# A planned one-core kernel: clearing, identity copy and running products moved in the opening, features due one step earlier, six float32 steps instead of eight

## The chip, the cores and the metric

The kernel runs on one core of one Trainium2 chip. The core has five engines with a program each: TensorE (PE in the profile), VectorE (DVE), ScalarE (ACT), GpSimd (POOL) and SyncE (SP), which here only issues transfers. The metric is the time of one execution on the device, in microseconds. Before the change the median of 3 runs is 601.78 us (600.33 to 602.82).

## The reference

Three layers follow each other. The first is a linear attention over 4 sequences of 768 tokens with 8 heads: in chunks, the decay between two tokens is the exponential of a difference of running sums of log a, and a state of 16 by 32 per head is carried from chunk to chunk. The other two are layers of 3072 tokens with 256 inputs, 2048 inner features and 256 outputs, one with softplus and one with a piecewise square.

```python
log_a = np.log(np.clip(a, 1e-06, 1.0))
cum = np.cumsum(la, axis=-1)
L = np.exp(cum[:, :, :, None] - cum[:, :, None, :])       # causal part only
y_intra = np.einsum('bhij,bhjd->bhid', CB * L, xc)
y_inter = np.einsum('bhin,bhnd->bhid', Cc, state) * decay_to_i[:, :, :, None]
state = decay_full[:, :, None, None] * state + np.sum(Bx, axis=2)
...
g = np.maximum(h, 0.0) + np.log1p(np.exp(-np.abs(h)))     # first layer, h = x @ w_in
g = np.where(pos, h, np.where(neg, 0.0, (h + beta) ** 2 / (4.0 * beta)))   # second
return (g @ w_out).astype(np.float32)
```

All inputs are float32 and the weights are given as 64-bit words, so that the kernel itself rebuilds float32 weights from two 32-bit halves.

## The kernel before

**Tiling.** The kernel takes its own chunks of 128 tokens: 6 chunks of 4 sequences, so 24 units, u = 4 c + b. A unit of chunk 0 makes its decays from the running sums (spread on TensorE, an exponential on ScalarE, L759). A unit of a later chunk loads rows of a and takes running products of them with one long scan on VectorE (`decay`, L757). `weigh` (L802) multiplies the scores by the decays, `out` (L826 to L838) makes outputs and state on TensorE, `evac` (L851) copies the output as high half xh on ScalarE, and `ready` (L860) subtracts it to give the low half xl on VectorE. A unit's xh and xl are its features.

**The layers as steps.** A step is an `up` (12 products of 256 columns, L893 to L895: xh by wih, xh by wil, xl by wih), an activation (`g`, L917), and a `down` into an accumulator. In chunks 0 and 1 a step takes 256 tokens (two units) and 256 of the 2048 inner features; later 512 tokens and 128 features. A `down` is either whole (L946: the float32 activation by the float32 weight, 4 products, which the trace shows as 8) or split: `g_hi` copies the high half (L500 on ScalarE or L502 on VectorE), `g_lo` subtracts (L932, on VectorE or GpSimd), and 12 products follow (L958). `whole(s)` says which: steps 0 to 7 before the change.

**The weights.** A piece of the first layer is loaded into one of 4 buffers st (two pieces go through the space of later features, raw), and rebuilt by w0 (L562 or L566), w1 (L574, ScalarE), w2 (L586), w3 (L598), a copy of the high half (L500 or L502) and `split_w` (L608) for the low half. wih, wil, woh and wol are the halves of the in and out weights. The names carry buffer numbers in the instruction lists: wih_75 to wih_82 are the eight pieces of w_in, woh_91 to woh_98 those of w_out.

**What sets the order.** Nothing is scheduled at run time. `program()` lists jobs with an engine, a cost, what they need, and the buffers they take and give back. `Jobs.order` walks through them: among the jobs that could start first on an engine it takes the one due earliest. A due time runs back from what follows; the job ("ready", u) has its own, `when(first step of its tokens - LEAD)`. Each engine then runs its list in that order, waiting in place. Short matmuls on an idle tile (L1034) are put in where the planner sees TensorE waiting in the opening; they write the bank of the job behind them.

**The opening (L987 to L1026, and the jobs of `a`).** GpSimd makes an identity (eye3), its seven copies (L1023), and the 0/1 patterns for the spread (L1018, L1022). `clip_a`, `log`, `sums` and `terms` (L640 to L657) make the running sums of chunk 0. `clip` (L687) writes the clipped a with zeros in its first column, `store` puts it in DRAM for the rows of the later chunks, and `runs` (L704, L707) takes running products of all of a, which `store_runs` and the loads `dec` bring to where `cd` (L777) and the state update need them, from chunk 1 on.

Of the kernel before, what the change touches and what calls it, by code (L numbers as in the profile page):

```python
# [14 lines left out]
NB, H, S, D, N = 4, 8, 768, 32, 16  # L15
Q = 128
# [6 lines left out]
PE, ACT, DVE, POOL, SP = "PE", "ACT", "DVE", "POOL", "SP"  # L23
# [167 lines left out]
def program():  # L191

    jobs = Jobs()
    add = jobs.add
# [29 lines left out]
    add("clip_load", SP, 400, due=-1e5, takes=["t"], size=98e3)  # L224
    add("clip", DVE, 350, needs=["clip_load", "sums"])
    add("store", SP, 800, needs=["clip"], size=98e3)
    add("runs", DVE, 1500, needs=["clip", ("columns", 1)])
    add("store_runs", SP, 1600, needs=["runs"], size=98e3, gives=["clip_load"])
    for c in range(1, NC):
        add(("dec", c), SP, 400 * DEC_DMAS, needs=["store_runs"], takes=["dec"], size=262e3)  # L230
    for u in range(NU):
        c, b = divmod(u, NB)
# [3 lines left out]
        if c == 0:  # L236
# [6 lines left out]
            decay = [("decay", u, 0), ("decay", u, 1)]  # L243
# [51 lines left out]
        if c < NC - 1:  # L295
            add(("sm", u), ACT, 500, needs=[("ready", u)])

# [87 lines left out]
]  # L385
WHOLE = 8
ACT_UNTIL = 120
# [9 lines left out]
    POOL: {"g_lo": 0.25, "weigh": 0.4, "sources": 1.0, "cd": 1.1, "sm": 0.6, "split_w": 0.4},  # L397
}
WEIGH_POOL = [3, 6]
PRELU = (0, 0)  # L400
# [9 lines left out]
STRETCH = 1.0  # L410
LEAD = 1
SPACE = 2
# [12 lines left out]
def tile_kernel(ctx: ExitStack, tc: tile.TileContext, a0, al, bc, ub, w_in, w_out, w2_in, w2_out, out):  # L425
# [7 lines left out]
    nc = tc.nc  # L433
# [195 lines left out]
    @job  # L629
    def a_load(engine):  # L630

        first = new(of("a_load"), F32, "first")
        tiles["a"] = [first[:, i * Q:(i + 1) * Q] for i in range(3)]
        nc.sync.dma_start(tiles["a"][0], a0.unsqueeze(0).to_broadcast([4, 32, Q]))
        nc.gpsimd.memset(tiles["a"][2], 1.0)

# [40 lines left out]
    @job  # L677
    def clip_load(engine):
        tiles["clip"] = new(of("clip_load"), F32, "clip0").rearrange("p (h i) -> p h i", h=4)[0:nr]
        nc.sync.dma_start(tiles["clip"], al.rearrange("r (h i) -> r h i", h=4))  # L680
        nc.gpsimd.memset(z_t[:, :, 0:1], 0.0)
        nc.gpsimd.memset(heads, 0.0)

# [303 lines left out]
    with tc.manual_schedule():  # L987
# [3 lines left out]
        for i in range(WARM):  # L991
# [13 lines left out]
            compare_op=ALU.is_ge, fill=-30000.0, base=0, channel_multiplier=-1,  # L1005
        )
        nc.vector.tensor_copy(eye16, eye3[:, 0])
        nc.vector.memset(low_bias, -0.5 + 7.5 * 2.0 ** -14)
# [13 lines left out]
        nc.gpsimd.tensor_copy(rows_t[r], of_seq[r].unsqueeze(2).to_broadcast([64, NB, Q]))  # L1022
        nc.gpsimd.tensor_copy(eye3[:, 1:], eye3[:, 0:1].to_broadcast([128, H - 1, Q]))  # L1023
        nc.vector.tensor_reduce(
# [61 lines left out]
```

## Time and profile before

| What | Value |
|---|---|
| Median of 3 runs | 601.78 us (600.33 to 602.82) |
| The profiled execution | 598.3 us, its span 596.6 us |
| TensorE busy | 587.1 us, 98% of the span |
| VectorE busy | 472.4 us, 79% |
| ScalarE busy | 255.1 us, 43% |
| GpSimd busy | 28.0 us, 5% |
| Granted TensorE clock | 1.0 of full speed throughout (2.4 GHz) |

The span runs from the first to the last instruction; the profiled execution's own time has 1.7 us around it. In the timeline a row is one instruction or a run of like ones: start, length, engine, line, output and inputs with buffer numbers left out, and in brackets how long the engine was idle before, and which instruction ended that. Rows of one engine overlap by a little where instructions are pipelined, so the distance of two starts is what one of them takes from the engine.

### The profile page before, as it was taken

To read this page: it belongs to the slowest core of one execution; us is meant where nothing else is said; L and a number is where in the kernel's file an instruction comes from. 1 tells how busy PE (TensorE), PEld (TensorE's weight loads), DVE (VectorE), ACT (ScalarE), POOL (GpSimd) and SP (SyncE) were. 2 spreads that over 40 slices of the span, in tenths; PEclk is the share of its full clock that TensorE was granted. 3 is DMA by queue.
4 is the path that set the end of the run, shared out by engine and by line. 5 is a ranking of instruction groups with operands and counts; after the bars stand their busy time and mean duration, and the time that the engine had idled before them with its cause. 6 is when DMAs were issued, how large, how long until landed. Compare 5 with 4: busy or idle time off the path is not lost.

```text
span 596.6 us, 9199 instructions
## 1 busy us (share of the span) xinstructions
PE 587.1 (98%) x3596; PEld 483.8 (81%) x3596; DVE 472.4 (79%) x787; ACT 255.1 (43%) x465; POOL 28.0 (5%) x31
## 2 busy tenths in 40 slices
PE   8799999999999999999999999999999999999997
PEld 3599998997787778778888888888888888888886
DVE  7999988856765764558998776679899899899895
ACT  5947534433433242336655876653222322322321
POOL 5442200000000000000000000000000000000000
PEclk9999999999999999999999999999999999999999
DMA  8995545502420320005430000000000000000000
GB/s 279 342 331 158 163 130 178 187 18 81 133 71 27 107 71 0 1 1 170 149 105 1 1 0 1 1 36 0 37 0 1 35 2 1 36 0 2 35 1 36
DMA packets 19863, 43.68 MB, mean 73 GB/s; under 512 B 1740, under 2 KB 2316, under 8 KB 19820
## 3 DMA queue, kind: packets, MB, share of 16 engines
q1 hardware_dynamic: 19820, 43.10, 21.7%
q8 instruction: 28, 0.46, 0.3%
q14 instruction: 15, 0.12, 0.1%
HBM read 39.75 MB, written 3.34 MB: 72 GB/s over the span
## 4 chain that ended last, share of the span: by engine, by line
PE 89%; DVE 7%; issue 2%; ACT 1%; DMA 1%; DVEq 0%
PE acc L958 42%; PE h L893 10%; PE h L894 10%; PE h L895 10%; PE acc L893 2%; PE acc L894 2%; PE acc L895 2%; PE y L831 2%; PE z L894 2%; PE z L895 2%; PE z L893 2%; PE y L793 2%; DVE w L598 1%; PE y L826 1%; DVE w L586 1%
## 5 line engine op out<-in xcount | busy, mean ns | idle before, releaser
L958 PE MATMUL acc<-gh,woh 128*128 128x512 f32 (+1 forms) x416 | 150.4, 369 | 0.0
L958 PE MATMUL acc<-gh,wol 128*128 128x512 f32 (+1 forms) x416 | 148.7, 365 | 0.0
L932 DVE TENSOR_TENSOR gl<-g,gh 128x512 fp32r<-128x512 f32 x181 | 124.7, 689 | 20.7 <-ACT gh L500 9.5
L893 PE MATMUL h<-xh,wih 128*128 128x512 f32 (+1 forms) x330 | 119.7, 363 | 0.0
L895 PE MATMUL h<-xl,wih 128*128 128x512 f32 (+1 forms) x330 | 117.5, 356 | 1.2 <-DVE xl L860 1.2
L894 PE MATMUL h<-xh,wil 128*128 128x512 f32 (+1 forms) x330 | 117.6, 356 | 0.2
L958 PE MATMUL acc<-gl,woh 128*128 128x512 f32 (+1 forms) x416 | 114.1, 365 | 0.0
L502 DVE CAST gh<-g 128x512 fp32r<-128x512 f32 x124 | 52.9, 426 | 56.2 <-ACT g L917 47.9
L958 PEld LDWEIGHTS acc<-gh,woh 128*128 128x128 f32 x416 | 78.4, 188 | 14.7 <-issue 0.9
L958 PEld LDWEIGHTS acc<-gh,wol 128*128 128x128 f32 x416 | 78.5, 189 | 12.2
L904 ACT ACTIVATE t<-h 128x512 f32<-128x512 f32 x63 | 37.8, 600 | 112.0 <-PE h L895 109.9
L958 PEld LDWEIGHTS acc<-gl,woh 128*128 128x128 f32 x416 | 73.3, 189 | 12.5
L893 PEld LDWEIGHTS h<-xh,wih 128*128 128x128 f32 x330 | 62.2, 189 | 11.9 <-issue 2.2
L895 PEld LDWEIGHTS h<-xl,wih 128*128 128x128 f32 x330 | 62.2, 189 | 10.3 <-DVE xl L860 1.4
L894 PEld LDWEIGHTS h<-xh,wil 128*128 128x128 f32 x330 | 62.3, 189 | 9.3 <-DVE wil L608 0.6
L917 ACT ACTIVATE g<-h 128x512 f32<-128x512 f32 x52 | 31.1, 598 | 73.2 <-PE h L895 65.2
L923 DVE SCALAR_TENSOR_TENSOR t<-t 128x512 f32<-128x512 f32 x72 | 49.6, 689 | 6.4 <-ACT t L904 6.1
L757 DVE TENSOR_TENSOR_SCAN ld<-ld,eye_t 128x1024 f32<-128x1024 f32 x20 | 46.7, 2335 | 1.0 <-DMA ld<-clip_z 1.0
L924 DVE TENSOR_TENSOR g<-h,t 128x512 f32<-128x512 f32 x63 | 43.6, 691 | 2.2
L500 ACT CAST gh<-g 128x512 fp32r<-128x512 f32 x60 | 37.2, 620 | 18.2 <-DVE g L924 16.8
L917 ACT ACTIVATE g<-acc 128x512 f32<-128x512 f32 x28 | 16.8, 599 | 38.3 <-PE acc L895 38.2
L893 PE MATMUL acc<-xh,wih 128*128 128x512 f32 (+1 forms) x68 | 24.1, 355 | 0.0
(148 smaller groups left out, 666.7 us busy)
## 6 DMA issues: line engine op xcount, KB each, us to landing
ld<-clip_z SPq DMA_DIRECT2D x20, 512.0 KB, 3.8
st<-in_w_in_dram SPq DMA_DIRECT2D x15, 512.0 KB, 6.8
st<-in_w_out_dram SPq DMA_DIRECT2D x15, 512.0 KB, 4.9
u<-in_ub_dram SPq DMA_DIRECT2D x24, 256.0 KB, 3.4
bc<-in_bc_dram SPq DMA_DIRECT2D x12, 384.0 KB, 3.4
out_dram<-dec SPq DMA_DIRECT2D x6, 256.0 KB, 2.2
dec<-clip_p SPq DMA_DIRECT2D x5, 256.0 KB
out_dram<-bc SPq DMA_DIRECT2D x5, 256.0 KB, 2.0
```

The costliest lines, as they stand in the source:

```text
L500: nc.scalar.copy(out, in_)
L502: engines[engine].tensor_copy(out, in_)
L757: nc.vector.tensor_tensor_scan(t, t, eye_t, 0.0, ALU.mult, ALU.add)
L893: nc.tensor.matmul(o, wh, xh[c][:, k, t0:t0 + n], start=(k == 0), stop=False)
L894: nc.tensor.matmul(o, wl, xh[c][:, k, t0:t0 + n], start=False, stop=False)
L895: nc.tensor.matmul(o, wh, xl[c][:, k, t0:t0 + n], start=False, stop=(k == 1))
L904: nc.scalar.activation(out=t, in_=ph, func=AF.Relu, bias=0.5, scale=0.5)
L917: nc.scalar.activation(out=g, in_=ph, func=AF.Softplus)
L923: nc.vector.scalar_tensor_tensor(out=t, in0=t, scalar=1.0, in1=t, op0=ALU.min, op1=ALU.mult)
L924: nc.vector.tensor_tensor(out=g, in0=ph, in1=t, op=ALU.max)
L932: engines[engine].tensor_tensor(out=mine("g_lo", s)[0], in0=mine("g", s)[0], in1=mine("g_hi", s)[0].bitcast(F32), op=ALU.subtract)
L958: nc.tensor.matmul(acc_t(s, e), w, g[:, j * n:(j + 1) * n], start=(begins(e, j) and g is gh and i == 0), stop=(fc + j == NFC - 1 and g is ...
```

## The change

GpSimd's clearing of z_t and heads (the two tiles of `clip` and `runs`, in the buffers dec) moves from the job `clip_load` to the opening, ahead of the patterns. The seven copies of the identity go from GpSimd to ScalarE, behind its first table load. The scan of `sums` reads its ones from the tile that the opening fills anyway, so one more clearing goes. `clip` needs the patterns of rows and columns to be written first, and `runs` needs the features of unit 1. In chunk 0 the job `sm` (L871, the state laid out for the next chunk's product) also needs the last decay of chunk 0. LEAD goes from 1 to 2, so the features of a step's tokens are due one step earlier, and WHOLE from 8 to 6, so steps 6 and 7 have a split `down`. Line numbers of the changed kernel differ by one or two from those of before.

```diff
--- before.py
+++ after.py
@@ -222,9 +222,9 @@
     for b in range(NB):
         add(("rows_of", b), DVE, 210, needs=["terms"] + [("columns", 1), ("rows_of", b - 1)] * (b == NB - 1), gives=["terms"] * (b == NB - 1))
     add("clip_load", SP, 400, due=-1e5, takes=["t"], size=98e3)
-    add("clip", DVE, 350, needs=["clip_load", "sums"])
+    add("clip", DVE, 350, needs=["clip_load", ("columns", 1)] + [("rows_of", b) for b in range(NB - 1)])
     add("store", SP, 800, needs=["clip"], size=98e3)
-    add("runs", DVE, 1500, needs=["clip", ("columns", 1)])
+    add("runs", DVE, 1500, needs=["clip", ("columns", 1)] + RUNS)
     add("store_runs", SP, 1600, needs=["runs"], size=98e3, gives=["clip_load"])
     for c in range(1, NC):
         add(("dec", c), SP, 400 * DEC_DMAS, needs=["store_runs"], takes=["dec"], size=262e3)
@@ -293,7 +293,7 @@
             gives=[("out", u)] + [("dec", c)] * (b == NB - 1 and c > 0),
         )
         if c < NC - 1:
-            add(("sm", u), ACT, 500, needs=[("ready", u)])
+            add(("sm", u), ACT, 500, needs=[("ready", u)] + [("decay", 3, 1)] * (u < NB))
 
 
     last_use, first_use = {}, {}
@@ -383,7 +383,7 @@
 ORDER = [
     (0, 0, 0, 4), (0, 1, 0, 4), (0, 0, 4, 4), (0, 1, 4, 4), (0, 0, 8, 8), (0, 1, 8, 8), (1, 0, 0, 16), (1, 1, 0, 16),
 ]
-WHOLE = 8
+WHOLE = 6
 ACT_UNTIL = 120
 H_MORE = 16
 H_ALL = 84
@@ -396,6 +396,7 @@
     DVE: {"w1": 1.1, "w2": 0.95, "w3": 0.95, "decay": 0.36, "split_w": 0.3, "g_lo": 0.1, "clip": 0.3, "runs": 0.3},
     POOL: {"g_lo": 0.25, "weigh": 0.4, "sources": 1.0, "cd": 1.1, "sm": 0.6, "split_w": 0.4},
 }
+RUNS = [("ready", 1)]
 WEIGH_POOL = [3, 6]
 PRELU = (0, 0)
 LOW_ACT = 1
@@ -408,7 +409,7 @@
 RATE = 330.0
 BEGIN = 14000.0
 STRETCH = 1.0
-LEAD = 1
+LEAD = 2
 SPACE = 2
 SHIFT = 2
 LAG = 1500
@@ -630,9 +631,8 @@
     def a_load(engine):
 
         first = new(of("a_load"), F32, "first")
-        tiles["a"] = [first[:, i * Q:(i + 1) * Q] for i in range(3)]
+        tiles["a"] = [first[:, i * Q:(i + 1) * Q] for i in range(2)] + [buf("ld", 4)[:, 0]]
         nc.sync.dma_start(tiles["a"][0], a0.unsqueeze(0).to_broadcast([4, 32, Q]))
-        nc.gpsimd.memset(tiles["a"][2], 1.0)
 
     @job
     def clip_a(engine):
@@ -678,8 +678,6 @@
     def clip_load(engine):
         tiles["clip"] = new(of("clip_load"), F32, "clip0").rearrange("p (h i) -> p h i", h=4)[0:nr]
         nc.sync.dma_start(tiles["clip"], al.rearrange("r (h i) -> r h i", h=4))
-        nc.gpsimd.memset(z_t[:, :, 0:1], 0.0)
-        nc.gpsimd.memset(heads, 0.0)
 
     @job
     def clip(engine):
@@ -1004,6 +1002,8 @@
             out=later, in_=idle, pattern=[[1, Q]],
             compare_op=ALU.is_ge, fill=-30000.0, base=0, channel_multiplier=-1,
         )
+        nc.gpsimd.memset(z_t[:, :, 0:1], 0.0)
+        nc.gpsimd.memset(heads, 0.0)
         nc.vector.tensor_copy(eye16, eye3[:, 0])
         nc.vector.memset(low_bias, -0.5 + 7.5 * 2.0 ** -14)
         nc.vector.tensor_reduce(out=of_head, in_=eye3[:, 0].rearrange("p (k h) -> p h k", h=H), axis=mybir.AxisListType.X, op=ALU.add)
@@ -1020,7 +1020,7 @@
             )
         r = slice(0, 64)
         nc.gpsimd.tensor_copy(rows_t[r], of_seq[r].unsqueeze(2).to_broadcast([64, NB, Q]))
-        nc.gpsimd.tensor_copy(eye3[:, 1:], eye3[:, 0:1].to_broadcast([128, H - 1, Q]))
+        nc.scalar.copy(eye3[:, 1:], eye3[:, 0:1].to_broadcast([128, H - 1, Q]))
         nc.vector.tensor_reduce(
             out=of_one, in_=eye3[:, 0].rearrange("p (k e n) -> p e k n", e=2, n=N), axis=mybir.AxisListType.XY, op=ALU.add
         )
```

VectorE, the opening, behind the terms of the running sums, in the kernel before. columns and rows are the patterns, dec_135 and dec_134 the tiles z_t and heads, clip_192 the running products (its scan is printed as SCALAR_TENSOR_TENSOR), ld the decays of a unit, w_271 the first piece of w_in and st_136 its load.

```order
L687 TENSOR_SCALAR dec_135<-clip_192 48x4x127
L664 TENSOR_TENSOR columns<-terms,of_69 64x512
L672 TENSOR_SCALAR rows<-terms,of_70 64x128 x2
L664 TENSOR_TENSOR columns<-terms,of_69 64x512
L672 TENSOR_SCALAR rows<-terms,of_70 64x128
L704 TENSOR_SCALAR dec_134<-clip_192 48x4
L707 SCALAR_TENSOR_TENSOR clip_192<-dec_135,dec_134 48x512
L802 TENSOR_TENSOR ld_119<-y,ld_119 128x512
L562 TENSOR_SCALAR w_271<-st_136 128x512
L802 TENSOR_TENSOR ld_119<-y,ld_119 128x512
L586 SCALAR_TENSOR_TENSOR w_271<-w_271,g 128x512
```

The same place in the changed kernel (w_254 is the first piece, its load again st_136):

```order
L672 TENSOR_SCALAR rows<-terms,of_70 64x128 x2
L664 TENSOR_TENSOR columns<-terms,of_69 64x512
L672 TENSOR_SCALAR rows<-terms,of_70 64x128 x2
L685 TENSOR_SCALAR dec_135<-clip_193 48x4x127
L563 TENSOR_SCALAR w_254<-st_136 128x512
L800 TENSOR_TENSOR ld_119<-y,ld_119 128x512
L800 TENSOR_TENSOR ld_120<-acc_214,ld_120 128x512
L800 TENSOR_TENSOR ld_119<-y,ld_119 128x512
L587 SCALAR_TENSOR_TENSOR w_254<-w_254,t 128x512
L599 SCALAR_TENSOR_TENSOR w_254<-st_136,w_254 128x512
```

The clipping moves behind the patterns, the running products leave this place (they stand 23 rows further on, behind the low half of unit 3), and the first conversion of the weight piece st_136 now stands ahead of the first weighing instead of behind it.

TensorE, the first `down`, in the kernel before. ld_122 with u_133 is the output of unit 3, gh by w_324 the `down` of step 0; ahead of them stands the output of unit 2, behind them the `up` of step 2 (wih_76).

```order
L831 MATMUL y<-ld_121,u_132 32x128 x8
L838 MATMUL y<-u_132,bt_314 32x64 x4
L946 MATMUL acc_216<-gh,w_324 128x256 x4
L831 MATMUL y<-ld_122,u_133 32x128 x8
L838 MATMUL y<-u_133,bt_253 32x64 x4
L893 MATMUL h_162<-xh_316,wih_76 128x256
L894 MATMUL h_162<-xh_316,wil_84 128x256
```

The same place in the changed kernel (w_352 is the same piece of w_out):

```order
L893 MATMUL h_160<-xl_306,wih_75 128x256
L829 MATMUL y<-ld_122,u_133 32x128 x8
L836 MATMUL y<-u_133,bt_250 32x64 x4
L944 MATMUL acc_238<-gh,w_352 128x256 x4
L891 MATMUL h_162<-xh_305,wih_76 128x256
L892 MATMUL h_162<-xh_305,wil_84 128x256
```

The output of unit 3 moves from behind the first `down` to ahead of it.

VectorE and TensorE where chunk 1 begins, in the kernel before. On VectorE xl_930 by y is the low half of a unit of chunk 1, first of unit 4 and then of unit 5, and the rows with ld and eye_t are the long scans.

```order
L982 TENSOR_TENSOR xl_317<-acc_216,xh_316 128x256
L860 TENSOR_TENSOR xl_930<-y,xh_929 128x2x128
L862 SCALAR_TENSOR_TENSOR s_66<-s_66,dec_134,y 128x64
L765 TENSOR_TENSOR bt_258<-u_133,ld_121 128x128
L777 TENSOR_TENSOR u_132<-u_132,dec_134 128x128
L502 CAST gh<-g 128x512
L777 TENSOR_TENSOR u_133<-u_133,dec_134 128x128
L932 TENSOR_TENSOR gl<-g,gh 128x512
L860 TENSOR_TENSOR xl_930<-y,xh_929 128x2x128
L862 SCALAR_TENSOR_TENSOR s_67<-s_67,dec_134,y 128x64
L757 SCALAR_TENSOR_TENSOR ld_123<-ld_123,eye_t 128x1024
L982 TENSOR_TENSOR xl_317<-acc_232,xh_316 128x256
```

VectorE at the same place in the changed kernel (xl_962 is the low half of chunk 1):

```order
L755 SCALAR_TENSOR_TENSOR ld_120<-ld_120,eye_t 128x1024
L980 TENSOR_TENSOR xl_306<-acc_238,xh_305 128x256
L858 TENSOR_TENSOR xl_962<-y,xh_961 128x2x128
L860 SCALAR_TENSOR_TENSOR s_66<-s_66,dec_134,y 128x64
L980 TENSOR_TENSOR xl_306<-acc_238,xh_305 128x256
L755 SCALAR_TENSOR_TENSOR ld_121<-ld_121,eye_t 128x1024
L858 TENSOR_TENSOR xl_962<-y,xh_961 128x2x128
L860 SCALAR_TENSOR_TENSOR s_67<-s_67,dec_134,y 128x64
L755 SCALAR_TENSOR_TENSOR ld_122<-ld_122,eye_t 128x1024
L755 SCALAR_TENSOR_TENSOR ld_123<-ld_123,eye_t 128x1024
```

Four of the long scans now stand around the low halves of chunk 1; before, two of these four stood some 30 rows ahead of the last weight piece's low half.

TensorE in the kernel before, ahead of the first `up` of chunk 1 (xh_929, xl_930); the 12 products by woh_98 and wol_106 are a whole split `down`, and right ahead of them stands the output of unit 5:

```order
L958 MATMUL acc_232<-gh,woh_98 128x256
L958 MATMUL acc_232<-gh,wol_106 128x256
L958 MATMUL acc_232<-gl,woh_98 128x256 x4
L893 MATMUL h_160<-xh_929,wih_75 128x256
L894 MATMUL h_160<-xh_929,wil_83 128x256
L895 MATMUL h_160<-xl_930,wih_75 128x256
```

TensorE at the same place in the changed kernel (xh_961, xl_962):

```order
L956 MATMUL acc_216<-gl,woh_98 128x256 x4
L824 MATMUL y<-u_131,sm_142 64x128 x4
L829 MATMUL y<-ld_119,u_131 32x128 x8
L836 MATMUL y<-u_131,bt_294 32x64 x4
L891 MATMUL h_160<-xh_961,wih_75 128x256
L892 MATMUL h_160<-xh_961,wil_83 128x256
L893 MATMUL h_160<-xl_962,wih_75 128x256
```

The `down` of the last step of chunk 0, which stood between the output of unit 5 and the first `up` of chunk 1, now stands ahead of that output.

## Rows read from the trace of the kernel before

**Rows 1.** The page, busy time and share of the span of each engine.

```profile
...
PE 587.1 (98%) x3596; PEld 483.8 (81%) x3596; DVE 472.4 (79%) x787; ACT 255.1 (43%) x465; POOL 28.0 (5%) x31
...
```

**Rows 2.** View of the waits, TensorE, whole run (us in total, times, longest).

```profile
...
PE acc L750 <- DVE rows L672: 1.7, 2, 1.5
PE acc L946 <- ACT gh L917: 1.6, 1, 1.6
PE h L895 <- DVE xl L860: 1.2, 1, 1.2
...
```

**Rows 3.** Timeline of TensorE, 19 to 34 us (start, length, line, operation, idle before).

```profile
...
23.37 1.99 PE L946 MATMUL acc<-gh,w 128*128 128x256 f32 x8 [1.60 <-ACT gh L917]
25.30 0.64 PE L831 MATMUL y<-ld,u 128*32 128x128 f32 x16
...
29.13 0.39 PE L895 MATMUL h<-xl,wih 128*128 128x256 f32 x1 [1.21 <-DVE xl L860]
...
30.42 3.62 PE L946 MATMUL acc<-gh,w 128*128 128x256 f32 x16
...
```

**Rows 4.** The chain that ended last, in order of time, middle of the run.

```profile
...
65.06 1.44 PE acc L958 x12
...
```

**Rows 5.** Timeline of VectorE, the opening.

```profile
...
3.98 1.71 DVE L640 TENSOR_SCALAR first<-first 128x128 f32<-128x128 f32 x1 [1.14 <-DMA first<-in_a_dram]
...
9.90 1.25 DVE L707 TENSOR_TENSOR_SCAN clip<-dec,dec 48x512 f32<-48x512 f32 x1
11.08 0.65 DVE L802 TENSOR_TENSOR ld<-y,ld 128x512 f32<-128x512 f32 x1
11.66 0.51 DVE L562 TENSOR_SCALAR w<-st 128x512 f32<-128x512 f32 x1
...
```

**Rows 6.** Timeline of GpSimd, the opening and the first product of a low half.

```profile
...
4.04 0.93 POOL L1023 COPY eye_t<-eye_t 128x896 f32<-128x896 f32 x1
...
5.09 0.52 POOL L682 MEMSET dec<- 48x512 f32 x1
...
55.19 1.70 POOL L932 TENSOR_TENSOR gl<-g,gh 128x512 fp32r<-128x512 f32 x1 [9.22 <-DVE w L562]
...
```

**Rows 7.** Timeline of SyncE, the issue of the first weight piece.

```profile
...
3.48 0.43 SPq L550 DMA_DIRECT2D st<-in_w_in_dram  x1
...
```

**Rows 8.** Transfers issued, 3.4 to 3.9 us (last number: us to landing).

```profile
...
st<-in_w_in_dram SPq DMA_DIRECT2D x1, 512.0 KB, 7.3
...
```

**Rows 9.** Timeline of ScalarE, 13 to 24 us.

```profile
...
13.07 0.78 ACT L574 ACTIVATE g<-st,low_bias 128x512 uint32<-128x512 uint32 x1 [0.29 <-DMA st<-in_w_in_dram]
...
22.72 0.60 ACT L917 ACTIVATE gh<-h 128x512 f32<-128x512 f32 x1
23.22 0.37 ACT L851 CAST xh<-y 128x256 fp32r<-128x256 f32 x1
...
```

**Rows 10.** Timeline of VectorE, 55 to 77 us.

```profile
...
55.67 1.78 DVE L608 TENSOR_TENSOR wil<-w,wih 128x512 fp32r<-128x512 f32 x1
...
62.76 0.68 DVE L608 TENSOR_TENSOR wil<-w,wih 128x512 fp32r<-128x512 f32 x1
63.36 0.68 DVE L932 TENSOR_TENSOR gl<-g,gh 128x512 fp32r<-128x512 f32 x1
...
68.77 2.27 DVE L757 TENSOR_TENSOR_SCAN ld<-ld,eye_t 128x1024 f32<-128x1024 f32 x1
...
76.47 0.42 DVE L860 TENSOR_TENSOR xl<-y,xh 128x256 fp32r<-128x256 f32 x1 [1.00 <-ACT xh L851]
...
```

**Rows 11.** Timeline of TensorE, 62 to 76 us.

```profile
...
62.95 0.38 PE L893 MATMUL h<-xh,wih 128*128 128x256 f32 x1
63.49 0.38 PE L894 MATMUL h<-xh,wil 128*128 128x256 f32 x1
...
75.93 0.38 PE L958 MATMUL acc<-gh,woh 128*128 128x256 f32 x1
...
```

**Rows 12.** Busy time by engine, granted clock and transfers, one stretch.

```profile
...
20.00:30.00 10.00, 7.19 (x87) 6.12 (x86) 9.60 (x15) 8.78 (x21) 3.42 (x3) 1.00 0.96 325
...
```

## The prediction

> **What bounds the kernel now.** I read the page first: TensorE is busy for 98% of the span [rows 1], so only its work and its few waits can move the end. The view of its waits names what it stood for, and its longest three lines all lie in the opening [rows 2]; none lies behind 29.13 us, where the last one ends [rows 3]. The granted clock is full in every stretch, as in the row of 20 to 30 us [rows 12]. In the chain of waits VectorE's weight conversions fill most of the time up to 63 us, and behind 65 us there are only products [rows 4]. Both views hold: from 29 us TensorE runs without a gap, and until 63 us VectorE just keeps ahead of it. The start of a product at 63.49 us, 0.54 us behind the one before it, comes right behind a low half that VectorE finished at 63.44 [rows 10, 11]: that is how narrow the lead is. So the time is the point at which TensorE's unbroken run begins, plus its work behind that, plus each place where VectorE falls behind.
>
> **The opening, and why most of it is hidden.** VectorE's first pass over a takes 1.71 us and ends at 5.69, right when GpSimd's string of copy and clears ends at 5.61 [rows 5, 6]. A pass over four times as many columns takes 0.51 (11.66, [rows 5]), so at least 1.2 us of the 1.71 is standing still. With the copy and clears out of the string, GpSimd has done its patterns at some 4.1 us and this pass should end near 4.4. The running products leave this place too, 1.25 us and a small pass [rows 5]. In all the decays can be ready 1.2 to 1.6 us earlier (the clipping leaves their path too), and the first weighing has 2.5 us or more less in front of it. The copy of the identity costs ScalarE between 0.60 us (half the columns, [rows 9]) and 1.05 us (scaled by 896/512), in the time in which it waits for a anyway: nothing.
>
> The Trainium skill, SBUF — State Buffer, section "SBUF: two separate sides", says that VectorE and GpSimd share a port pair as an exclusive lock for one instruction, so the second waits for the first only. By that the first pass would have gone on behind the GpSimd pass that was running at its start, ahead of the copy of 4.04 [rows 6], and the move would give the opening nothing. The trace disagrees, since it ended behind GpSimd's whole string; I go by the trace.
>
> But VectorE's next step in the changed list is the first conversion of the first weight piece, and the weighings stand behind it. That load is issued at 3.48 us [rows 7] and lands 7.3 us later [rows 8], at 10.8 us; the six issues up to it are the same in both kernels, so it should land there again. Before, the conversion ran at 11.66, behind one weighing at 11.08 [rows 5]. So VectorE waits some 2 us, until 10.8, and does its first weighing at 11.2, where it did it before: the whole gain of the opening is stood out in this one wait. ScalarE has the same landing ahead of the last four exponentials.
>
> **TensorE's run, term by term** (minus is time saved).
>
> First softplus. ScalarE is the path to it. Its list from the landing to the softplus at 22.72 has one long conversion of 0.78 and one pass of about 0.60 less, one copy of about 0.60 and a feature copy of 0.37 with a small one of 0.2 more [rows 9]: -0.2. It takes the piece at its landing, where before exponentials stood ahead: -0.2 by my count. The second weight piece now comes behind two unit loads, 512 KB more; at the 325 GB/s of [rows 12] that is 1.6 us on its 13.07 us [rows 9], where ScalarE arrives some 0.3 us earlier; and the idle products now write the bank of the outputs and wait for unit 1's low half, so that unit 2's output comes near 19.6 and ScalarE waits 0.3 for it. That is 0.6 against 0.29 before [rows 9]: +0.3. Sum -0.1, bounds -1.0 and +0.4.
>
> Output of unit 3. Its larger part ran at 25.30 for 0.64, behind the first `down` [rows 3]; now it stands in front, in the 1.60 us that TensorE waits for the softplus: -0.64, or 0 if its weighing is late.
>
> Unit 3's low half. With the output earlier, ScalarE copies it right behind the softplus, and VectorE has it near 23.7, where the `up` that needs it starts at about 26: the wait of 1.21 goes [rows 3]: -1.21, or 0.
>
> Two steps. Sixteen whole products take 3.62 us, so a step at most 1.81 [rows 3], a split one 1.44 [rows 4]. Overlap takes some 0.1 off the first. -0.27 each, -0.55 together; bounds -0.74 and -0.4.
>
> VectorE's lead. From the first conversion to the low half of unit 5 the changed list has 62 passes of 512 columns at 0.60 (0.68 less the overlap of two starts, [rows 10]), 4 scans at 2.2 [rows 10], 23 short passes at about 0.34 (the row of 0.42 less the same overlap), the running products at 1.43 and 5 small ones at 0.2: 37.2 + 8.8 + 7.8 + 1.4 + 1.0 = 56.2 us. Each GpSimd product that runs beside it costs it 1.10 us (1.78 against 0.68 for one operation, while GpSimd's product of 55.19 ran, [rows 6, 10]). There are two of w_out and four of g here, against four and two before: 6.6 us, or 5.5 if the last falls beside a scan. Waits for ScalarE in the first features about 1.7, GpSimd's weighing 0.5. So VectorE is done with unit 5's low half at 10.8 + 56.2 + 6.6 + 2.2 = 75.8 us, 74.7 in the better case. The same count by order for the last low half of w_in (wil_90) gives some 60 to 61 us, against TensorE's need at 60.5: in balance, where before it missed by 0.42 (the 0.54 of [rows 11] less a product's 0.12). I take -0.3 for that, bounds -0.6 and +1.2.
>
> Entry of chunk 1. Before, a whole `down` of 1.44 us from 75.93 lay between unit 5's output and the `up` that reads it, and the low half came at 76.47 to 76.89 under that cover [rows 10, 11]. Now nothing lies between: after the output come ScalarE's copy of 0.37 [rows 9], VectorE's 0.42 and the two hand-overs, and only two products of 0.12 run meanwhile: +0.75 at least. With the sums above the `up` would want that low half at 77.4 - 0.1 - 0.64 - 1.21 - 0.55 - 0.3 = 74.6 plus 0.24 (77.4 is 75.93 plus the 1.44), and the chain without cover gives it at 75.6, VectorE's sum at 74.7 to 75.8: +0.75, bounds +0.5 and +2.3 (a scan of 2.27 right in front, [rows 10]). Two more scans follow, but the next low half of g is wanted 6 to 7 us later and VectorE needs 5.4 for what is ahead of it: nothing.
>
> Sum: -0.1 - 0.64 - 1.21 - 0.55 - 0.3 + 0.75 = -2.05, say -2.1. The profiled execution had 596.6 of span and 1.7 around it, 598.3; the changed one comes to 594.5 and 596.2. The median of the runs shown is 3.5 above the profiled one, so I carry the difference over: 601.8 - 2.1 = 599.7 us.
>
> **Rivals.** (1) Larger gain: VectorE is earlier than my sum (GpSimd's products cost less, or fall beside scans), chunk 1 opens with the least wait of 0.5, the balance gives -0.6 and the softplus -1.0. -1.0 - 0.64 - 1.21 - 0.74 - 0.6 + 0.5 = -3.7: 598.1. For it: a GpSimd product cost VectorE anything up to 1.1. Against: ScalarE's path has no obvious slack.
>
> (2) Everything is stood out: the gain up to 31 us is real, but VectorE, whose list to the same place is as long as before (56.2 against 55.5 us), takes it back as waits for low halves between 54 and 75 us. Then the time is set by VectorE alone, which starts 0.3 earlier: 601.0, between -1 and +1. For it: VectorE is busy from 10 to 73 us and the lead at 63 us is nil [rows 11]. Against: two scans have left the stretch ahead of wil_90.
>
> (3) Slower: the scans put around unit 5's low half make VectorE miss it. The `up` wants it at 74.8 and without this wait the gain is 2.8, so all is gone when VectorE delivers after 77.6. Two scans stretched by 1.1 each by a GpSimd product, and waits for ScalarE 1 us longer than counted, would bring 75.8 to 79.0: 1.4 past that point, 603.2. For it: the order puts a 2.27 us scan right in front. Against: it needs two things at once.
>
> **Numbers.** Forecast 0.52, rival 1 0.24, rival 2 0.14, rival 3 0.10. Predicted 599.7; the range 597.2 to 602.4 leaves out about a tenth above and a tenth below; the forecast's own range is 598.5 to 600.9. A change of 0.5%, 3.0 us, is about what a measurement of this kernel can tell, with runs 2.5 us apart. Faster by more than that (below 598.8): rival 1 nearly whole and a fifth of the forecast, 0.33. Slower by more: part of rival 3, 0.07. Within: 0.60.
>
> **What would show it.** The first pass over a short (0.4 us) and ended near 4.4; VectorE and ScalarE idle until about 10.8 for the first weight piece; the first weighing near 11.2; the first softplus near 22.6; no wait of TensorE for unit 3's low half, its unbroken run from about 26; the first product with unit 5's low half 0.5 us or more late, behind a scan on VectorE. Wrong would be: the weight piece landing well before 10 us, VectorE idle between 30 and 60 us, or waits of TensorE beyond 80 us.

## The result: 596.5 us, below the range, and the profile after

The changed kernel takes 596.54 us in the median of 4 executions (596.07 to 597.06); the kernel before, run beside it, 602.30 (600.33 to 602.88). The ratio is 0.9911 with a 95% interval of 0.9889 to 0.9933. The prediction was 599.7, the range 597.2 to 602.4: the gain is over twice the one forecast.

The two profiled executions tell less. Before: 598.3 us with a span of 596.6. After: 597.06 with 595.3. That is a gain of 1.2 us, where the medians are 5.8 apart. So most of the gain doesn't stand in the two traces, and the first question was what the usual execution of the kernel before does that its profiled one did not.

The page of the changed kernel, the row that answers to [rows 1]:

```profile
PE 583.7 (98%) x3598; PEld 482.6 (81%) x3598; DVE 469.2 (79%) x789; ACT 258.6 (43%) x469; POOL 38.0 (6%) x28
```

GpSimd has fewer instructions and 10 us more of busy time. TensorE's waits in the changed kernel, which answer to [rows 2]:

```profile
PE y L1034 <- DVE xl L858: 1.7, 1, 1.7
PE y L1034 <- DVE ld L800: 1.6, 1, 1.6
PE acc L944 <- ACT gh L915: 1.3, 1, 1.3
PE y L791 <- DMA bc<-in_bc_dram: 1.1, 1, 1.1
...
PE acc L956 <- POOL gl L930: 0.8, 1, 0.8
PE h L891 <- ACT xh L849: 0.5, 1, 0.5
```

The wait for unit 3's low half is gone. The lines of L1034 are waits of the short products on an idle tile, for the first low halves and weighings. New behind the opening are 0.5 us where chunk 1 begins, and one that no part of the prediction named: 0.8 us for GpSimd's product of the low half of g. The timeline of the changed kernel (start, length, engine, line; in brackets the idle time before), the opening and the place of these two waits:

```profile
3.75 0.65 DVE L640 TENSOR_SCALAR first<-first 128x128 f32<-128x128 f32 x1 [0.85 <-DMA first<-in_a_dram]
10.42 0.43 DVE L563 TENSOR_SCALAR w<-st 128x512 f32<-128x512 f32 x1 [1.66 <-DMA st<-in_w_in_dram]
10.76 0.68 DVE L800 TENSOR_TENSOR ld<-y,ld 128x512 f32<-128x512 f32 x1
18.23 1.67 PE L1034 MATMUL y<-idle 128*128 128x512 bf16 x7 [1.68 <-DVE xl L858]
20.66 0.37 ACT L849 CAST xh<-y 128x256 fp32r<-128x256 f32 x1 [1.15 <-PE y L836]
22.14 0.64 PE L829 MATMUL y<-ld,u 128*32 128x128 f32 x16
23.54 0.60 ACT L915 ACTIVATE gh<-h 128x512 f32<-128x512 f32 x1
24.19 1.99 PE L944 MATMUL acc<-gh,w 128*128 128x256 f32 x8 [1.29 <-ACT gh L915]
28.89 3.62 PE L944 MATMUL acc<-gh,w 128*128 128x256 f32 x16
30.27 13.20 POOL L609 TENSOR_TENSOR wol<-w,woh 128x512 fp32r<-128x512 f32 x1 [1.03 <-ACT woh L501]
50.83 8.51 POOL L930 TENSOR_TENSOR gl<-g,gh 128x512 fp32r<-128x512 f32 x1 [7.36 <-ACT gh L501]
57.53 0.68 DVE L599 SCALAR_TENSOR_TENSOR w<-st,w 128x512 uint32<-128x512 uint32 x1
59.39 0.74 PE L956 MATMUL acc<-gl,woh 128*128 128x256 f32 x4 [0.80 <-POOL gl L930]
60.51 1.65 DVE L609 TENSOR_TENSOR wil<-w,wih 128x512 fp32r<-128x512 f32 x1 [2.30 <-ACT wih L501]
75.89 0.39 PE L891 MATMUL h<-xh,wih 128*128 128x256 f32 x1 [0.49 <-ACT xh L849]
```

The two whole `down`s that ran at 30.42 in [rows 3] run at 28.89, 1.53 us earlier. The first product of chunk 1 runs at 75.89; before, it came behind the `down` of 75.93 [rows 11], at 77.46, 1.57 us later. From there to the end both traces need nearly the same: 519.1 us before, 519.4 after. And GpSimd products of the shape that took 1.70 us in [rows 6] take 8.51 and 13.20 here. (Spans on GpSimd are rough, but TensorE's wait for the end of the one of 8.51 is not.) The trace of the kernel before has a long one as well, at 40.13, which TensorE didn't wait for (below it, the first product of chunk 1):

```profile
40.13 5.84 POOL L608 TENSOR_TENSOR wol<-w,woh 128x512 fp32r<-128x512 f32 x1 [7.79 <-ACT woh L500]
77.46 0.28 PE L893 MATMUL h<-xh,wih 128*128 128x256 f32 x1
```

### The profile page after: what moved, and what is told of

It is laid out like the page before. It is cut to its first block, busy times and chain, and to the rows that moved or that the text cites. A ratio compares the mean times of both kernels' runs of the same rounds, so it can differ in the third digit from the quotient of the medians.

```text
span 595.3 us, 9221 instructions
## 1 busy us (share of the span) xinstructions
PE 583.7 (98%) x3598; PEld 482.6 (81%) x3598; DVE 469.2 (79%) x789; ACT 258.6 (43%) x469; POOL 38.0 (6%) x28
## 4 chain that ended last, share of the span: by engine, by line
PE 94%; POOL 1%; ACT 1%; DMA 1%; DVE 1%; issue 1%; SPq 0%; ACTq 0%
PE acc L956 43%; PE h L891 11%; PE h L893 10%; PE h L892 10%; PE y L829 2%; PE acc L891 2%; PE acc L892 2%; PE acc L893 2%; PE z L892 2%; PE z L893 2%; PE z L891 2%; PE acc L944 2%; PE y L791 2%; POOL gl L930 1%; PE y L824 1%; DMA st<-in_w_in_dram 1%
## 5 line engine op out<-in xcount | busy, mean ns | idle before, releaser
L956 PE MATMUL acc<-gh,woh 128*128 128x512 f32 (+1 forms) x424 | 152.4, 367 | 0.0
L956 PE MATMUL acc<-gh,wol 128*128 128x512 f32 (+1 forms) x424 | 150.6, 363 | 0.0
L930 DVE TENSOR_TENSOR gl<-g,gh 128x512 fp32r<-128x512 f32 x182 | 125.9, 692 | 21.7 <-ACT gh L501 10.8
L956 PE MATMUL acc<-gl,woh 128*128 128x512 f32 (+1 forms) x424 | 115.5, 363 | 0.8 <-POOL gl L930 0.8
L956 PEld LDWEIGHTS acc<-gh,woh 128*128 128x128 f32 x424 | 79.9, 188 | 14.8 <-issue 0.9
L956 PEld LDWEIGHTS acc<-gh,wol 128*128 128x128 f32 x424 | 80.0, 189 | 12.2
L915 ACT ACTIVATE g<-h 128x512 f32<-128x512 f32 x55 | 32.9, 597 | 74.8 <-PE h L893 67.4
L501 ACT CAST gh<-g 128x512 fp32r<-128x512 f32 x65 | 40.4, 621 | 21.9 <-DVE g L922 16.8
L755 DVE TENSOR_TENSOR_SCAN ld<-ld,eye_t 128x1024 f32<-128x1024 f32 x20 | 45.5, 2281 | 0.2 <-DMA ld<-clip_z 0.2
```

Of the source, the lines that this page charges most:

```text
L501: nc.scalar.copy(out, in_)
L755: nc.vector.tensor_tensor_scan(t, t, eye_t, 0.0, ALU.mult, ALU.add)
L915: nc.scalar.activation(out=g, in_=ph, func=AF.Softplus)
L930: engines[engine].tensor_tensor(out=mine("g_lo", s)[0], in0=mine("g", s)[0], in1=mine("g_hi", s)[0].bitcast(F32), op=ALU.subtract)
L956: nc.tensor.matmul(acc_t(s, e), w, g[:, j * n:(j + 1) * n], start=(begins(e, j) and g is gh and i == 0), stop=(fc + j == NFC - 1 and g is ...
```

## The experiments

Two theories. A: the usual execution of before loses a race between VectorE and GpSimd that its profiled one had won. GpSimd's product of a low half is held off by VectorE's unbroken stream, TensorE waits for it, and the changed plan mostly moves these products out of the way. B: VectorE's lead is what was short, as the prediction had it, and the terms were too small. A ratio below is to the kernel before on the same chip, with its 95% interval.

**1. The parts of the change, and the kernel before again.** e1 is the kernel before, unchanged. e2 is before with the opening's edits alone:

```diff
-        nc.gpsimd.memset(tiles["a"][2], 1.0)
-        nc.gpsimd.memset(z_t[:, :, 0:1], 0.0)
-        nc.gpsimd.memset(heads, 0.0)
...
-        nc.gpsimd.tensor_copy(eye3[:, 1:], eye3[:, 0:1].to_broadcast([128, H - 1, Q]))
+        nc.scalar.copy(eye3[:, 1:], eye3[:, 0:1].to_broadcast([128, H - 1, Q]))
```

(with the two clearings put ahead of the patterns). e3 is before with all the rest of the change, the plan. e4 is the changed kernel with eight whole steps:

```diff
-WHOLE = 6
+WHOLE = 8
```

e1: 

> The kernel before, unchanged, to see how far its executions differ and where. Its one profiled execution took 598.3 us, its timed ones 600.3 to 602.9. If the loss of the timed ones is a wait that comes and goes (VectorE's lead over TensorE, nil at 63 us), this run's times spread over 598 to 603 again and a profile of a slower one shows TensorE waiting 2 to 4 us longer than the first profile did, between 29 and 75 us. If a profile as such makes this kernel faster, the profile shows the first one's waits again, within 0.5 us.

e2: 

> Only the opening: the clears first on GpSimd, the identity copied by ScalarE, the ones of the scan from the filled tile; the planned order is that of before. If the 3.5 us between my sum and the measured gain sit in the opening (GpSimd's string holding VectorE for a varying time), this gives 597.5 to 599.5. If the opening is stood out behind the first weight piece, as predicted, or behind what follows, it is within 1 us of before: 601 to 603; VectorE's first pass takes 0.4 to 0.7 us instead of 1.71 either way.

e3: 

> Only the plan: running products and clipping later, the features due one step earlier, six float32 steps, the state jobs later; the opening's own instructions stay as before. If the gain is in the plan (TensorE's terms and a better lead of VectorE), this gives 596.5 to 598.5 and spreads by about 1 us. If it needs the opening, 599.5 to 602.

e4: 

> The changed kernel with eight float32 steps instead of six. By my sum two steps are worth 0.55 us of TensorE's work and two low halves more on VectorE: 597.1 if only TensorE's work counts. If the six steps matter through VectorE's or GpSimd's work (four low-half products of w_out go back to GpSimd), anything from 595.5 to 599.5.

Measured: e1 601.82 us (598.13 to 604.27), ratio 1.0006 [0.9980, 1.0032]; e2 601.01, ratio 1.0002 [0.9982, 1.0022]; e3 596.68, ratio 0.9929 [0.9901, 0.9957]; e4 598.32, ratio 0.9956 [0.9935, 0.9976]. The opening by itself leaves the median where it was, the plan gives all, and of it the two steps are worth 1.8 us (598.32 against 596.54). But e2 doesn't show that the opening's edits save nothing. In its trace VectorE's first weighing and TensorE's first `down` come 1.3 and 1.0 us earlier than in e1 (11.09 and 23.20), and then TensorE waits 2.72 us for GpSimd, as in e1 below, with a low clock behind it:

```profile
9.78 0.66 DVE L799 TENSOR_TENSOR ld<-y,ld 128x512 f32<-128x512 f32 x1
22.22 1.99 PE L943 MATMUL acc<-gh,w 128*128 128x256 f32 x8 [1.61 <-ACT gh L914]
61.32 0.75 PE L955 MATMUL acc<-gl,woh 128*128 128x256 f32 x4 [2.72 <-POOL gl L929]
64.00:66.00 2.00, 2.00 (x17) 1.20 (x17) 1.61 (x4) 0.14 (x1) 0.00 (x0) 0.50 0.00 0
```

(The last row is a stretch: start:end, length, busy time of PE, PEld, DVE, ACT, POOL, then the granted clock, the DMA share and GB/s; the clock here is 0.50 of full speed.) None of e2's 12 executions is below 600.47 us, where 16 of 98 of the kernel before are below 599. So what the opening saves is lost again behind 58 us.

The profiled execution of e1 took 600.41 us. TensorE's longest wait in it, and the timeline of the place:

```profile
PE acc L958 <- POOL gl L932: 2.7, 1, 2.7
```

```profile
54.60 0.42 DVE L562 TENSOR_SCALAR w<-st 128x512 f32<-128x512 f32 x1
54.92 8.57 POOL L932 TENSOR_TENSOR gl<-g,gh 128x512 fp32r<-128x512 f32 x2 [11.57 <-ACT gh L500]
54.94 0.68 DVE L598 SCALAR_TENSOR_TENSOR w<-st,w 128x512 uint32<-128x512 uint32 x1
55.54 0.68 DVE L608 TENSOR_TENSOR wil<-w,wih 128x512 fp32r<-128x512 f32 x1
...
60.42 0.68 DVE L608 TENSOR_TENSOR wil<-w,wih 128x512 fp32r<-128x512 f32 x1
62.28 0.75 PE L958 MATMUL acc<-gl,woh 128*128 128x256 f32 x4 [2.72 <-POOL gl L932]
64.39 0.48 PE L793 MATMUL y<-bc 32*128 32x256 f32 x2
64.68 0.69 DVE L932 TENSOR_TENSOR gl<-g,gh 128x512 fp32r<-128x512 f32 x1 [3.57 <-ACT gh L500]
```

It is the same program as in [rows 6, 10]. There GpSimd's product was done in 1.70 us, and VectorE's L608 beside it took 1.78. Here L608 takes 0.68, VectorE runs on without a gap until 61.1, and GpSimd's first product is done only when VectorE has stopped, 1.2 us later. TensorE stands for 2.72 us, and ScalarE, which VectorE needs for its next pass, stands 3.51 us for the same product. This is what theory A asks for. The Trainium skill, SBUF — State Buffer, "SBUF: two separate sides", has the shared port pair go for a whole instruction to whichever of the two starts first, so a product would be blocked for one instruction. The trace doesn't bear that out: the product stays behind eleven of VectorE's instructions that start after it (54.94 to 60.42).

**2. The race taken out.** The low halves of g that were GpSimd's go to VectorE, at the same places: in before (e5) and in the changed kernel (e6). e7 moves the low halves of the weights in `split_w` too, so that GpSimd multiplies none of the layers' tiles.

```diff
-        engines[engine].tensor_tensor(
+        nc.vector.tensor_tensor(
```

e5: 

> The kernel before with the products of the low half of g (L932) given to VectorE at the same places, so that GpSimd has none of them. Theory A (the time of before is set by a race: GpSimd's low-half product is held off by VectorE's stream for 6.5 to 8.6 us and TensorE waits 2.7 us for it in most executions): the wait of TensorE for gl goes, the time falls to 597 to 598.5 us, and its executions lie within about 1 us instead of 5. Theory B (VectorE's lead is what is short, and its three more products cost that lead): 601 to 604 us, spread as before.

e6: 

> The changed kernel with its low-half products of g on VectorE at the same places. Theory A: the 0.8 us that TensorE still waits for GpSimd's product of gl in the changed kernel goes, and the time falls from 596.5 to 595.3 to 596.3 us. Theory B (VectorE's lead is what is short in the opening): the added products on VectorE make TensorE wait for xl and xh instead, 597 to 599 us.

e7: 

> The changed kernel with GpSimd's products for the low halves of g and of the output weights all on VectorE, so that GpSimd multiplies nothing beside VectorE (one took 13.20 us in the changed kernel's trace). Theory A: VectorE is nowhere held, TensorE's waits for GpSimd are gone, 595 to 596.5 us. Theory B: VectorE has two or three more products of about 0.5 to 1 us in the stretch where its lead is short, and the time is 597.5 to 600 us.

Measured: e5 597.45 us (597.36 to 598.54), ratio 0.9951 [0.9932, 0.9970]; e6 595.84 (595.37 to 597.77), ratio 0.9922 [0.9895, 0.9950]; e7 595.30 (594.71 to 595.65), ratio 0.9907 [0.9875, 0.9940]. TensorE's waits in e5, all of them over 0.2 us:

```profile
PE acc L946 <- ACT gh L917: 1.6, 1, 1.6
PE h L895 <- DVE xl L860: 1.2, 1, 1.2
PE h L992 <- DVE idle L990: 1.1, 1, 1.1
PE acc L750 <- DVE rows L672: 1.0, 1, 1.0
```

One line of code, which gives VectorE three more products, takes the kernel before to 4.4 us below e1's median (3.0 below the executions of before beside it, which had 600.40), and its executions lie within 1.2 us where e1's spread over 6.1. That is also 0.7 us below the executions of before that had won (598.1). The opening's waits are those of [rows 2] still. Theory A holds, and B falls as the cause of the spread and of most of the gain. With the race out of both, the rest of the change is worth 597.45 - 595.84 = 1.6 us; the prediction's terms made 2.1. e7 beats both kernels.

**3. The plan's edits one by one.** e8 is before with `WHOLE = 6` alone. e9 is before with

```diff
-            add(("sm", u), ACT, 500, needs=[("ready", u)])
+            add(("sm", u), ACT, 500, needs=[("ready", u)] + [("decay", 3, 1)] * (u < NB))
...
-LEAD = 1
+LEAD = 2
```

e10 is before with the new needs of `clip` and `runs` alone:

```diff
-    add("clip", DVE, 350, needs=["clip_load", "sums"])
+    add("clip", DVE, 350, needs=["clip_load", ("columns", 1)] + [("rows_of", b) for b in range(NB - 1)])
...
-    add("runs", DVE, 1500, needs=["clip", ("columns", 1)])
+    add("runs", DVE, 1500, needs=["clip", ("columns", 1)] + RUNS)
```

and e11 is e6 with `WHOLE = 8`.

e8: 

> The kernel before with the one number WHOLE = 6 in place of 8. GpSimd then has four products of the low half of g where it had three. Theory A (the race for gl sets the time of before): the placing of those products against VectorE's stream decides, four of them leave the race in, and the median lies between 598 and 601.5 us with a spread over 2 us. Theory C (the two steps are the gain by themselves, 1.8 us as between eight and six steps in the changed kernel): 599.5 to 600.5 us as a shift of the whole distribution. By the prediction's term of 0.55 us it would be 601.3 us.

e9: 

> The kernel before with LEAD = 2 and the need of the softmax on the decays, nothing else of the change: eight steps, three products of the low half of g on GpSimd as before. By the prediction this brings unit 3's output and low half forward, so that TensorE's wait of 1.2 us for xl and the output behind the first down go: -1.2 to -1.9 us, at most. Theory A (race for gl): those two waits go, yet the race stays with its wait of 2.7 us, so the median is 599.5 to 601.5 us and the spread over 2 us. If this edit carries the change: 596.5 to 598 us.

e10: 

> The kernel before with the new needs of the clipping and of the running products alone. Its plan leaves GpSimd one product of the low half of g instead of three. Theory A: with a single such product the race is mostly out, no wait of 2.7 us for gl, 597 to 599 us with a spread near 1 us. Theory B (what is gained is VectorE's lead in the opening): VectorE now has two more products and the waits of before in the opening stay, 601 to 602.5 us.

e11: 

> The changed kernel with WHOLE = 8 and all low-half products of g on VectorE, so that the race is out; against the same with six steps (595.8 us) it prices the two steps alone. If the 1.8 us between eight and six steps (598.3 and 596.5) is TensorE's own work (its busy time differed by 1.2 us) and small waits for VectorE: 597.2 to 597.8 us. If the prediction's 0.55 us was right and the rest lay in the race for gl: 596.2 to 596.6 us.

Measured: e8 600.31 us (599.41 to 602.38), ratio 0.9986 [0.9967, 1.0006]; e9 599.07 (599.05 to 599.78), ratio 0.9961 [0.9947, 0.9976]; e10 596.61 (596.52 to 597.89), ratio 0.9923 [0.9894, 0.9952]; e11 597.27 (596.12 to 599.48), ratio 0.9932 [0.9911, 0.9954]. e8 is no clear change: its fastest execution is 1.3 us above the fastest of before beside it, its median 1.4 below. So the two steps alone don't shift the whole distribution, and a spread of 3.0 us stays, as theory A had it. e9 missed my expectation: it doesn't spread. Its two products are held off in its trace too, but TensorE waits only 1.0 us:

```profile
54.69 9.73 POOL L932 TENSOR_TENSOR gl<-g,gh 128x512 fp32r<-128x512 f32 x2 [12.02 <-ACT gh L500]
63.22 0.74 PE L958 MATMUL acc<-gl,woh 128*128 128x256 f32 x4 [1.00 <-POOL gl L932]
```

Its 12 executions lie within 0.7 us, so I take the race as lost in each of them, which one profile can't show; the spread of before comes from a race that goes either way. e10 is the surprise: two edits, in which the prediction saw no time of their own beyond the opening, bring all that the whole change brings. They don't touch the low halves of g. But the planner, with other due times on VectorE, leaves GpSimd one such product in place of three, and that one is done in 1.34 us, VectorE being the one that is held. The timeline of e10:

```profile
57.09 1.34 POOL L933 TENSOR_TENSOR gl<-g,gh 128x512 fp32r<-128x512 f32 x1 [17.50 <-ACT gh L501]
57.20 1.78 DVE L587 SCALAR_TENSOR_TENSOR w<-w,t 128x512 uint32<-128x512 uint32 x1
```

The two steps, priced between e11 and e6 without the race, are worth 597.27 - 595.84 = 1.4 us by medians; the executions of the two overlap. Sixteen whole products less are 3.62 us and two split `down`s more 2.9, so 0.74 of it is TensorE's own work, the upper bound of the prediction's term; the rest are waits that only eight steps have. TensorE's waits in e11 (the profile of e4 has the same two):

```profile
PE h L892 <- DVE wil L609: 0.4, 1, 0.4
...
PE h L893 <- DVE xl L858: 0.2, 1, 0.2
```

**4. What is still open: executions of 601.5 to 603 us.** Two more profiles of the kernel before, and e14, which is e10 with its one product of g moved to VectorE as in e5.

e12: 

> The kernel before, unchanged, for one more look with a profile. Theory A (race for gl): its time and TensorE's wait for GpSimd's gl go together, as in the two looks so far (598.3 us with no such wait, 600.4 with 2.7): an execution of 598.0 to 598.7 has none, one of 600 to 601 has about 2.7, one of 601.5 to 603 has over 3 us or a second such wait. Theory B (something outside the products of gl): a time of 601.5 to 603 with a wait for gl of 2.7 or less, and the rest in other waits or in TensorE's own work.

e13: 

> The kernel before, unchanged, a second time in this call, with a profile; about half of its executions lie between 601.5 and 603 us. Theory A: the same relation of time and wait as for the look before this one: below 598.7 no wait for gl, 600 to 601 some 2.7 us, 601.5 to 603 over 3 us or two such waits. Theory B: over 601.5 with no more than 2.7 us for gl.

e14: 

> The new needs of the clipping and the running products alone (596.6 us by itself), with the one product of gl that GpSimd keeps given to VectorE; beside it stands the kernel before with its three products moved in the same way, 597.45 us. Theory A (the gain of that edit is almost all that it takes two products of gl out of the race): 596.5 to 597.6 us, so that only 0 to 1 us of its 5 us are its own. Theory B (the edit gains by VectorE's lead in the opening and the race matters little to it): a product more on VectorE costs, 597.8 to 599 us.

Measured: e12 602.94 us, e13 598.04 us, e14 596.87 (596.51 to 598.79), ratio 0.9938 [0.9915, 0.9960]. In e13 no wait for GpSimd; its timeline goes as in [rows 6, 10]:

```profile
54.98 1.70 POOL L932 TENSOR_TENSOR gl<-g,gh 128x512 fp32r<-128x512 f32 x1 [9.22 <-DVE w L562]
55.45 1.77 DVE L608 TENSOR_TENSOR wil<-w,wih 128x512 fp32r<-128x512 f32 x1
```

e12 has the wait of e1, 2.66 us, and no second one. The other 2.5 us between 602.94 and 600.41 are neither of the things theory A named. The stretches of e12 (the granted clock is the third number from the end), and the products behind the wait:

```profile
8.00:10.00 2.00, 1.40 (x5) 0.67 (x5) 1.86 (x7) 0.60 (x1) 0.08 (x1) 0.70 1.00 364
10.00:12.00 2.00, 2.00 (x7) 0.95 (x6) 1.87 (x3) 1.32 (x3) 1.79 (x3) 0.50 1.05 405
...
62.00:64.00 2.00, 0.65 (x3) 0.65 (x4) 0.17 (x1) 0.67 (x2) 2.00 (x2) 0.85 0.81 247
64.00:65.00 1.00, 1.00 (x7) 1.00 (x6) 0.00 (x0) 1.00 (x2) 0.54 (x1) 0.50 0.94 340
65.00:66.00 1.00, 1.00 (x6) 1.00 (x6) 0.26 (x1) 1.00 (x3) 0.00 (x0) 0.50 0.20 76
66.00:67.00 1.00, 1.00 (x10) 0.85 (x8) 1.00 (x3) 0.17 (x1) 0.00 (x0) 0.59 0.00 0
```

```profile
63.35 1.21 PE L958 MATMUL acc<-gl,woh 128*128 128x256 f32 x4 [2.66 <-POOL gl L932]
...
66.97 0.48 PE L793 MATMUL y<-bc 32*128 32x256 f32 x2
```

TensorE stood for 2.66 us, and right behind that its granted clock was at the lower of its two levels (0.50, 1.2 GHz) until past 66 us. From the end of the wait to L793 it needs 3.62 us in e12; e1, at full clock, needs 64.39 - 62.28 = 2.11. That is 1.5 us. Another fall, at 8 to 12 us, goes with the other 1.0: the same GpSimd product starts at 55.99 in e12 and 54.92 in e1, where the clock was full. So the long executions are three things on top of 598.1: the wait (+2.3), the clock behind the wait (+1.5), the clock in the opening (+1.0). The fall in the opening doesn't need the race: the profiled execution of e11, where GpSimd has no product of g, has a clock of 0.62 and 0.53 between 14 and 18 us and takes 599.48, 2.2 above its median.

The 98 timed executions of before fall into groups that fit this, with the mean granted clock of each beside its time. The causes in the last column are seen in the profiles of 598.0, 598.3, 600.4 and 602.9 us and, for the other groups, inferred from the sum:

| us | executions | mean granted clock, most often | causes |
|---|---|---|---|
| 598.1 to 598.9 | 16 | 1.0 | none |
| 599.2 to 599.4 | 8 | 0.996 to 0.997 | one fall of the clock |
| 600.3 to 601.0 | 17 | 1.0 | the wait |
| 601.5 to 602.2 | 33 | 0.997 | the wait and one fall |
| 602.4 to 604.3 | 24 | 0.994 | the wait and two falls |

By that three executions in four have the wait. e5 leaves out the products and has neither the wait nor, in ten of twelve executions, a fall (597.4 to 597.7); its other two take 598.5 at 0.996. Between the medians of e5 and e14 the new needs are worth 597.45 - 596.87 = 0.6 us of their own, which is less than either run's spread; the other 4.5 of the 5.1 that they bring in e10 (601.72 to 596.61) are the race and what comes with it.

## Why the prediction was wrong

**The step that failed** is the last one of its sum: "The median of the runs shown is 3.5 above the profiled one, so I carry the difference over". That difference was not a constant of the measurement. It was a wait of TensorE of 2.7 us, in most cases with a fall of the clock, that most executions of the kernel before have and its profiled one had not. The change shortens the wait to 0.8 us, and none of its four executions has a mean clock below 1.0: the changed kernel's profiled execution is the longest of its four, not 3.5 us below the median. Shown by the four profiles of before and by e5.

Behind it stands a second step: "Each GpSimd product that runs beside it costs it 1.10 us". That was one outcome of a race, read as the only one, and priced for VectorE alone. In the other, VectorE loses nothing while GpSimd's product takes until VectorE pauses, and no rival of the prediction had TensorE wait for GpSimd. The product of 5.84 us in the trace of before was a sign of it that the prediction passed over. The changed kernel loses that race as well; but there VectorE stands from 58.2 us, waiting for ScalarE, which waits for the same product (1.19 us), so TensorE's wait is 0.8 us, where in e1 VectorE ran on to 61.1. No term of the prediction had that: the larger part of the gain is luck as far as the prediction goes.

The other steps, by their own terms:

- The opening gives nothing. Right for the changed order: the first pass over a ends at 4.40, the weight piece lands at 10.42, and the first weighing is at 10.76 (forecast 4.4, 10.8 and 11.2). e3, which has the changed order without the opening's edits, weighs first at 10.41 (the row below) and takes 596.68 us against 596.54. In the order of before the same edits do bring the first `down` 1.0 us forward; e2's ratio of 1.0002 hides that behind the race.

```profile
10.41 0.67 DVE L803 TENSOR_TENSOR ld<-y,ld 128x512 f32<-128x512 f32 x1
```

- First softplus: forecast -0.1 with bounds of -1.0 and +0.4, measured +0.8 (23.54 against 22.72 in [rows 9]), outside the bounds. ScalarE's wait for the output of unit 2 is 1.15 us, where I counted 0.3: an idle product holds TensorE until 18.23 for unit 1's low half, and that output ends at 20.6, where I had 19.6.
- Output of unit 3 ahead of the first `down`, and unit 3's low half: right; it stands at 22.14 and the wait of 1.2 is gone. With the softplus late, 1.53 us of the forecast 1.95 are there at 28.89.
- Two steps and VectorE's lead: together forecast at -0.85, measured -1.4 (e11, e6); the two are one thing, since the waits for wil and xl come with steps 6 and 7.
- Entry of chunk 1: forecast +0.75, bounds +0.5 and +2.3; the wait is 0.49. The low half is there in time and the scan of 73.10 does no harm.
- Sum: -1.24 between the profiled executions; without the 0.8 us for GpSimd it is -2.0, and between e5 and e6, without the race, -1.6 in medians and -2.1 in profiled executions (597.45, 595.38), for a forecast of -2.1. The mechanism was seen and the sum nearly sized, in part by luck, since the softplus came 0.9 late and the two steps gave some 0.5 more, and in the trace that lacked what mattered.

## What to carry to other kernels

When the profiled execution is several us below the median of the timed ones, take a second profile before any sum: the difference can be a wait that the trace doesn't have, and a change can remove it. A product on GpSimd beside a busy VectorE should be priced from both outcomes, VectorE held for a microsecond or GpSimd held for many microseconds, and it should not be one that TensorE waits for. Here a line that gave those products to VectorE was worth 3.0 us of the median of the kernel before against the executions beside it, 4.4 against e1's, and 0.7 of the changed one (596.54 to 595.84), and with the low halves of the weights 1.2 (595.30).

## What the runs showed of the hardware

- The same program's GpSimd product took 1.70 us in two profiles and was held for over 7 us in two others. In the first two it started 0.14 and 0.15 us into a VectorE instruction of 0.68; in the other two 0.32 into one of 0.42. No rule came of that: in e10 a product that started 0.50 us into one of 0.68 won, in the changed kernel one at 0.33 lost.
- The loser can wait very long: 13.20 us for one product of 512 columns in the changed kernel, from 30.27, while VectorE's instructions of 0.68 beside it kept their length. It got in without a pause of VectorE: behind a scan of 2.27 at 40.12, where VectorE's next, a copy of 0.42, took 1.39. The product of 5.84 in the trace of before ended in the same way, behind a scan at 42.61 with VectorE's next taking 1.70. Why there is not shown.
- A stand of TensorE of 2.7 us was followed by the lower clock in one profile of before (e12) and in e2, and not in another of before (e1); the 0.8 us of the changed kernel was followed by none. Which of the two comes behind 2.7 us stays open.
